# A new order for three chained stages, a mask made first, and three weight copies on another engine

## The chip, the cores and the metric

The kernel runs on one core of one Trainium2 chip. That core has TensorE (PE, matrix products into PSUM banks), VectorE (DVE), ScalarE (ACT), GpSimd (POOL) and SyncE (SP, which here only issues transfers); 16 DMA engines move data between HBM and the on-chip SBUF. The metric is the device time of the whole program in microseconds (us), the median of several executions. A time that goes down is an improvement.

## The reference

Three stages, the output of each the input of the next. The weights are float64, everything else float32.

```python
# attention: q, k, v of 4 x 8 x 576 x 64, a causal window of 64
scores = np.matmul(q, k.transpose(0, 1, 3, 2)) / np.sqrt(D)
mask = (rel >= 0) & (rel < 64)                       # rel = row - column
scores = np.where(mask, scores, -1e9)
attn = np.exp(scores - max); attn = attn / (sum + 1e-9)
x = np.matmul(attn, v)                               # -> 2304 x 512
# relu squared: 512 -> 2048 -> 512
h = np.maximum(x @ w_in, 0.0); x = h * h @ w_out
# SoLU: 512 -> 1024 -> 512
h = x @ w2_in
solu = h * softmax(h)
ln = (solu - mean) / np.sqrt(var + 1e-6) * g_ln
out = ln @ w2_out
```

## The kernel before

**Tiling.** The 2304 tokens are cut into blocks of 64. Two blocks make a *unit* of attention: a mask product and score products (`ps_s`, L417 and L436), the largest score of each row (`nmax`, L440 to L446, DVE), exponentials (`e`, L451, ACT), the division by the sums (L456 to L461), transposes (`ps_p`, L477 and L479), a copy (`pt`, L497, ACT) and the values (`ps_v`, L517 to L522). The feed-forward stage then goes through `ps_h` (L691, or L936 in later passes) and `ps_y` (L707, L1070, L1256). It works in passes over groups of tokens; the later passes and the third stage replace eight block products by seven, with sums and differences of blocks on DVE (`wf`, `y`, `g`, `gx`, `xx`, `ws`, `w2i`, `w2x`). Each float32 operand is split into a high and a low part, and each product is three products (high by high, high by low, low by high). The SoLU stage takes tokens in pairs of tiles: `pair2` makes `ps_h` at L1546 (42 matmuls of 512 columns for a pair), then the exponentials and the norm make `lnT` (L1696), and `ps_o` (L1707, 48 matmuls for a pair) gives the output, scaled and stored.

**Weights.** A block of float64 weights (128 x 512) comes by DMA as half-words (`wraw`, L236, issued by SP). A *half-word copy* moves each top half-word to its place in a zeroed buffer (`top`, a ring of two places for the feed-forward weights): by DVE (L263) for those with `i < TOPS`, else by ACT (L265). DVE then shifts the rest in (L268), ACT makes the high part (L284), DVE the low part (L287). The weights of the first product are called a0, a1, ... (`in_w_in`, then `wa`), those of the second b0, b1, ... (`in_w_out`, then `wb`). Products of the first pass can start when a0, its high and low parts and the first unit's values are there.

**Order.** Every piece of work is a task of a `Plan` (from L27): an engine, an estimated length, a rank, what it must follow, which buffers it takes and gives, and `late`, an allowance after its end (for a transfer, until its data can be used). `run` places on each step the task that can start first, and of these the one of lowest rank; a table `SHIFT` adds a number to the rank of single tasks. `emit` then writes the tasks in the order of their planned starts, and nothing is reordered afterwards: an engine that waits for one instruction holds up all that stand behind it on that engine, and the same is true of SP's and ACT's transfers. `late` and the table are numbers of the plan alone; they change no instruction, only places.

**Filling.** 51 matmuls of `ones` (`ps_warm`, L1782) have the highest rank of all, so that the plan puts them where it sees TensorE idle: 36 as one group, then 15 single ones. Their result isn't used.

**The start.** Constants are made first: `ident` and `mask` by POOL, `ident_b`, `lower` and `mask_b` by DVE (L175 to L183). `mask_b` goes into every mask product; `lower` is used from the third unit on. `top` is zeroed by POOL (L256), just before the first half-word copy needs it.

**The end.** The last output tile is scaled in two halves into two buffers, one by ACT (L1721), one by DVE (L1723), and each half is stored by a transfer of its own, one issued by SP and one by ACT (L1727). All other tiles are scaled whole by ACT (L1712).

Of the kernel before, what the change touches and what calls it, by code (L numbers as in the profile page):

```python
# [20 lines left out]
P = 128  # L21
# [5 lines left out]
class Plan:  # L27
# [10 lines left out]
    SHIFT = {0: 13.59, 3: 4.48, 4: -11.32, 22: -7.17, 37: 14.79, 71: -15.08, 162: -5.57, 188: 6.06, 192: -3.28, 195: 10.82, 198: 10.82, 202: -1.28,  # L38
# [69 lines left out]
def kernel(  # L108
# [68 lines left out]
    V.memset(mhalf, -0.5)  # L177
    lower = const.tile([P, 2 * BLK], F32, name="lower")
    V.tensor_scalar(out=lower, in0=mask, scalar1=0.0, scalar2=1e29, op0=ALU.min, op1=ALU.mult)
    mask_b = const.tile([P, 2 * BLK], BF16, name="mask_b")  # L180
    V.tensor_scalar(out=mask_b, in0=mask, scalar1=0.0, scalar2=8.0, op0=ALU.min, op1=ALU.mult)
    ident_b = const.tile([P, P], BF16, name="ident_b")
    V.tensor_copy(ident_b, ident)  # L183
# [21 lines left out]
    with ExitStack() as c1:  # L205
# [151 lines left out]
        def attention(n, rank, after=()):  # L357
# [186 lines left out]
            if n == 0:  # L544
                lqs = [add("SP", 1.1, rank - 6, lambda h=h: load_qk(h), take=qk * (h == 0), late=2.0, at=0.7) for h in range(2)]
# [300 lines left out]
        def w_operands(t, j, rank, after):  # L846
# [9 lines left out]
            def kept(o, k):  # L856
                nc.sync.dma_start(out=wo_dram[j][:, k], in_=o["t"].bitcast(F32))
# [48 lines left out]
            kept_wo[j] = [add("SP", 1.6, rank + WOS, lambda o=o, k=k: kept(o, k), [x], late=2.5) for k, (o, x) in enumerate(((V_, v), (Y, y)))]  # L906
# [5 lines left out]
        def pair1(t, j, at, unit, held, begins_after=()):  # L912
# [91 lines left out]
            for x, kk, f, k in (("c22", 2 * j + 1, f22, 6), ("u3", 2 * j, f21, 8)):  # L1004
                f = squared(Named({}, o, x), N, rank(k) + 14.3, [f], False, False)
                r_ready[t, kk] = add("SP", 0.8, rank(k) + 3, lambda x=x, kk=kk: store(x, kk), [f], late=LATE_R if t == 2 else 2.2, give=["wm"])
# [829 lines left out]
```

## Time and profile before

| | us |
|---|---|
| median of 3 executions | 630.67 (630.58 to 631.52) |
| the profiled execution's own time | 631.49 |
| its span, first to last instruction | 629.7 |
| TensorE busy in the span | 621.6 (99%) |
| VectorE busy | 484.6 (77%) |
| ScalarE busy | 434.8 (69%) |
| GpSimd busy | 45.3 (7%) |
| mean granted clock of TensorE | 1.000 |

The profiled execution took 631.49 us, of which 629.7 us lie between its first and its last instruction; the other 1.8 us lie around the span. Its own time is near the highest of the three others. Matmuls are pipelined and their ends are modelled, so rows of TensorE overlap a little: the distance between two starts says how long a group held the engine. In the trace a name in front of the arrow is what is written, the names behind it what is read; "idle before" is the engine's idle time ahead of an instruction, and the name behind it what came last. "SPq" is the queue of transfers that SP issues.

### The profile page before, as it was taken

Reading aid. Unit: us, or ns where it says so; the run is one execution under the profiler, and the core shown is the slowest. Engines: PE = TensorE matmul, PEld = TensorE weight load, DVE = VectorE, ACT = ScalarE, POOL = GpSimd, SP = SyncE. Lnnn points to the kernel's source line nnn. Section 1 sums busy time; section 2 is a strip of 40 time slices with the busy share of each in tenths; the row PEclk is TensorE's granted clock in tenths of the full one; section 3 lists DMA queues with packets and bytes.
Section 4 is the critical chain, followed back from the end, with each engine's and each line's share of the span. In section 5 each row is a group of like instructions: output and inputs, shape, how many; then the busy total and the mean of one; then the engine's idle time right before and its main releaser. Section 6 shows DMA issues by size and latency. Waiting matters only on the chain.

```text
span 629.7 us, 11572 instructions
## 1 busy us (share of the span) xinstructions
PE 621.6 (99%) x4009; PEld 523.7 (83%) x4009; DVE 484.6 (77%) x1129; ACT 434.8 (69%) x985; POOL 45.3 (7%) x80
## 2 busy tenths in 40 slices
PE   8999999999999999999999999999999999999998
PEld 4798878889999999998888887778778788888886
DVE  5999897497967652587899998998688976686440
ACT  5879785677877674638677767774688875776451
POOL 1000000001221110000000000000001010110010
DMA  8888979447899998946767557964166565532351
GB/s 274 287 305 278 310 252 326 128 173 264 247 351 312 336 304 271 337 155 230 236 251 263 203 195 235 328 208 138 68 184 206 181 199 167 197 137 86 116 184 50
DMA packets 85451, 141.27 MB, mean 224 GB/s; under 512 B 7824, under 2 KB 49552, under 8 KB 85392
## 3 DMA queue, kind: packets, MB, share of 16 engines
q1 hardware_dynamic: 84704, 140.14, 66.3%
q8 instruction: 31, 0.51, 0.3%
q10 hardware_dynamic: 688, 0.39, 0.2%
q14 instruction: 28, 0.23, 0.1%
HBM read 90.69 MB, written 49.81 MB: 223 GB/s over the span
## 4 chain that ended last, share of the span: by engine, by line
PE 86%; DVE 5%; DMA 4%; ACT 3%; issue 1%; SPq 1%; POOL 0%; ACTq 0%; DVEq 0%; POOLq 0%
PE ps_h L936 22%; PE ps_o L1707 14%; PE ps_y L1070 10%; PE ps_h L1546 10%; PE ps_y L1256 10%; PE ps_y L707 7%; PE ps_h L691 6%; PE ps_s L436 3%; PE ps_v L519 2%; PE ps_warm L1782 1%; DMA l<-t_dram 1%; DMA kt<-in_k 1%; DMA r_dram<-u 1%; DMA t_dram<-h 1%; PE ps_v L522 1%
## 5 line engine op out<-in xcount | busy, mean ns | idle before, releaser
L1707 PE MATMUL ps_o<-w2o,lnT 128*128 128x512 f32 x432 | 99.1, 389 | 0.0
L1707 PEld LDWEIGHTS ps_o<-w2o,lnT 128*128 128x128 f32 x432 | 81.1, 188 | 16.9
L1256 PE MATMUL ps_y<-g,wb 128*128 128x384 f32 x384 | 71.3, 336 | 0.4 <-ACT y L655 0.4
L1256 PEld LDWEIGHTS ps_y<-g,wb 128*128 128x128 f32 x384 | 66.6, 188 | 1.4 <-ACT y L655 0.7
L1546 PE MATMUL ps_h<-w2i,xx 128*128 128x512 f32 x243 | 62.8, 391 | 0.0
L1070 PE MATMUL ps_y<-g,wb 128*128 128x512 f32 x234 | 58.3, 391 | 1.1 <-DVE y L1157 1.0
L1546 PEld LDWEIGHTS ps_h<-w2i,xx 128*128 128x128 f32 x243 | 45.6, 188 | 9.6
L1070 PEld LDWEIGHTS ps_y<-g,wb 128*128 128x128 f32 x234 | 43.7, 188 | 11.4 <-DVE y L1157 1.4
L936 PE MATMUL ps_h<-xa,wo 128*128 128x512 f32 (+1 forms) x192 | 52.7, 369 | 0.0
L936 PE MATMUL ps_h<-xb,wo 128*128 128x384 f32 (+1 forms) x192 | 51.3, 358 | 0.0
L707 PE MATMUL ps_y<-g,wb 128*128 128x512 f32 (+1 forms) x240 | 48.2, 352 | 0.1
L691 PE MATMUL ps_h<-x,wa 128*128 128x512 f32 (+1 forms) x240 | 47.3, 351 | 0.0
L936 PE MATMUL ps_h<-xo,wo 128*128 128x512 f32 (+1 forms) x128 | 47.3, 369 | 0.0
L451 ACT ACTIVATE e<-e,nmax 128x128 f32<-128x128 f32 x112 | 43.3, 390 | 2.2 <-DVE nmax L440 2.2
L707 PEld LDWEIGHTS ps_y<-g,wb 128*128 128x128 f32 x240 | 38.5, 189 | 6.6 <-issue 0.7
L691 PEld LDWEIGHTS ps_h<-x,wa 128*128 128x128 f32 x240 | 38.5, 189 | 6.0 <-ACT g L637 0.2
L936 PEld LDWEIGHTS ps_h<-xa,wo 128*128 128x128 f32 x192 | 35.3, 188 | 5.2 <-DVE u L622 0.4
L1696 ACT ACTIVATE lnT<-l 128x512 fp32r<-128x512 f32 x36 | 22.2, 627 | 23.0 <-PE ps_o L1707 23.0
L1546 PE MATMUL ps_h<-w2x,xx 128*128 128x512 f32 x135 | 37.0, 393 | 0.9 <-ACT u L1560 0.7
L936 PEld LDWEIGHTS ps_h<-xb,wo 128*128 128x128 f32 x192 | 34.5, 188 | 3.9 <-issue 0.7
L640 DVE TENSOR_TENSOR g<-r,g 128x384 fp32r<-128x384 f32 (+2 forms) x36 | 20.4, 570 | 21.7 <-ACT g L637 21.7
L461 POOL TENSOR_TENSOR e<-e,sums 128x512 f32<-128x512 f32 x16 | 18.5, 1179 | 205.0 <-PE ps_h L936 141.9
(182 smaller groups left out, 1267.7 us busy)
## 6 DMA issues: line engine op xcount, KB each, us to landing
wraw<-in_w_in SPq DMA_DIRECT2D x24, 511.8 KB, 5.3
wraw<-in_w_out SPq DMA_DIRECT2D x24, 511.8 KB, 4.8
vt<-in_v SPq DMA_DIRECT2D x32, 256.0 KB, 4.3
wo_dram<-wo SPq DMA_DIRECT2D x16, 512.0 KB, 5.4
wo<-wo_dram SPq DMA_DIRECT2D x16, 512.0 KB, 4.9
t_dram<-h SPq DMA_DIRECT2D x16, 512.0 KB, 2.9
l<-t_dram SPq DMA_DIRECT2D x64, 128.0 KB, 2.9
kt<-in_k SPq DMA_DIRECT2D x16, 384.0 KB, 5.2
```

Source lines behind the costliest of these rows:

```text
L436: T.matmul(to, qt[rows, i, hp, :], kt[rows, keys, hp, :], start=not begins, stop=not begins or hp == hps[-1])
L451: S.activation(out=o["er"][:, a, w], in_=s, func=AF.Exp, scale=SCALE if begins else -1.0, bias=o["nmax"][:, a, w : w + 1], accum_out=o["su ...
L461: eng.tensor_tensor(out=o["er"][:, a], in0=o["er"][:, a], in1=o["sums"][:, a].unsqueeze(2).to_broadcast([P, HP, W]), op=ALU.mult)
L640: V.tensor_tensor(out=o["g"][:, 1, :N], in0=o["r"], in1=o["g"][:, 0, :N].bitcast(F32), op=ALU.subtract)
L691: T.matmul(ps[:, :N], wa[kk][:, wi, c * P : c * P + P], xs[t][:, xi, c, n0:n1], start=n == 0, stop=n == 3 * DC - 1)
L707: T.matmul(acc[t, 0][d][:, n0:n1], wb[kk][:, wi, d * P : d * P + P], o["g"][:, xi, :N], start=kk == 0 and n == 0 and n0 == 0, stop=last an ...
L936: T.matmul(to[:, :N], w["t"][:, wi, off + c * P : off + c * P + P], (lo if xi else hi)()[:, c], start=begins and m == 0, stop=m == 5, skip ...
L1070: T.matmul(acc[name][d][:, :N], wb[kk][:, wi, col + d * P : col + d * P + P], q["g"][:, xi, :N], start=j == 0 and n == 0 and name not in ( ...
L1256: T.matmul(acc[t, half][d][:, :N], wb[kk][:, wi, d * P : d * P + P], q["g"][:, xi, :N], start=pos == 0 and n == 0, stop=pos == KF - 1 and ...
L1546: T.matmul(o[bank], o["xx", k][:, xi, at : at + P], w2i[w, r][wi][0](), start=begins and m == 0, stop=m == 5, skip_group_check=True)
L1696: S.activation(out=parts2(o["l", hf][:, 0]), in_=turned2(hf), func=AF.Copy)
L1707: T.matmul(o["o"], o["l", hf][:, xi, kk % 4, :], w2o[kk][:, wi, :], start=kk == 0 and n == 0, stop=kk == KF2 - 1 and n == 2)
```

## The change

The function of the program is the same, and so are the counts of every form of matmul. What changes:

- **The table `SHIFT`** is replaced by another with half as many entries, and four kinds of `late` are changed (the loads of q and k of the first unit, and several stores). Together they put most of the work of all engines in another order.
- **Constants:** `ident_b`, `mask_b`, `lower` in that order, and `top` is created and zeroed up front, by DVE instead of POOL.
- **Half-word copies** of a0, a1 and b0 go from DVE to ACT. The place in the ring of `top` is now taken from a list of free ones and given back after the shift.
- **The end:** the last tile is scaled whole by ACT and stored in two halves, still by SP's and ACT's queues.

```diff
-    SHIFT = {0: 13.59, 3: 4.48, 4: -11.32, 22: -7.17, 37: 14.79, 71: -15.08, 162: -5.57, 188: 6.06, 192: -3.28, 195: 10.82, 198: 10.82, 202: -1.28,
+    SHIFT = {0: 23.49, 10: 1.29, 28: -4.64, 214: 8.42, 331: -39.05, 389: 14.27, 467: -9.61, 473: -42.13, 501: 3.17, 563: 26.76, 1037: -4.85,
...
+    ident_b = const.tile([P, P], BF16, name="ident_b")
+    V.tensor_copy(ident_b, ident)
+    mask_b = const.tile([P, 2 * BLK], BF16, name="mask_b")
+    V.tensor_scalar(out=mask_b, in0=mask, scalar1=0.0, scalar2=8.0, op0=ALU.min, op1=ALU.mult)
     lower = const.tile([P, 2 * BLK], F32, name="lower")
     V.tensor_scalar(out=lower, in0=mask, scalar1=0.0, scalar2=1e29, op0=ALU.min, op1=ALU.mult)
-    mask_b = const.tile([P, 2 * BLK], BF16, name="mask_b")
...
-        tops, turns = [], [0]
+        tops, turns = [x_p.tile([P, 2, 512], F32, tag="xc", name="top", bufs=1)], [0, 1]
+        V.memset(tops[0], 0.0)
...
-            by_dve = ringed and i < TOPS
+            by_dve = ringed and (1 if kind == "b" else 2) <= i < TOPS
...
-                    if not tops:
-                        tops.append(x_p.tile([P, 2, 512], F32, tag="xc", name="top", bufs=1))
-                        G.memset(tops[0], 0.0)
-                    o["t"] = tops[0][:, turns[0] % 2]
-                    turns[0] += 1
+                    o["turn"] = turns.pop(0)
+                    o["t"] = tops[0][:, o["turn"]]
...
+                if ringed:
+                    turns.append(o["turn"])
...
-                lqs = [add("SP", 1.1, rank - 6, lambda h=h: load_qk(h), take=qk * (h == 0), late=2.0, at=0.7) for h in range(2)]
+                lqs = [add("SP", 1.1, rank - 6, lambda h=h: load_qk(h), take=qk * (h == 0), late=1.8, at=0.7) for h in range(2)]
...
-                if b == 0:
-                    S.activation(out=o["y", b][:, cols], in_=o["o"][:, cols], func=AF.Copy, scale=o["rstd"])
-                else:
-                    V.tensor_scalar(out=o["y", b][:, cols], in0=o["o"][:, cols], scalar1=o["rstd"], scalar2=None, op0=ALU.mult)
...
+            a = add("ACT", 0.59, rank_o, scaled, [a, r], take=["r"], give=["a"])
             if k == 1 and p["last"]:
-                b = add("ACT", 0.35, rank_o, lambda: scaled_half(0), [a, r], take=["r"])
-                c = add("DVE", 0.35, rank_o, lambda: scaled_half(1), [a, r], take=["r"], give=["a"])
-                add("SP", 0.5, rank_o, lambda: store_half(0), [b], late=2.0, give=["r"])
-                add("ACT", 0.1, rank_o, lambda: store_half(1), [c], late=2.0, give=["r"])
+                add("SP", 0.5, rank_o, lambda: store_half(0), [a], late=2.0, give=["r"])
+                add("ACT", 0.1, rank_o, lambda: store_half(1), [a], late=2.0)
```

What this moves shows best in the order of instructions. The new kernel's line numbers are 4 lower from the constants on, and up to 14 lower at the end.

**SP's loads at the start.** Before, SP issues a0 (`in_w_in`), the v of unit 0, b0 (`in_w_out`), a1, then unit 2's q and k, a2, the v of unit 1:

```order
L236 DMA wraw<-in_w_in 128x2047
L401 DMA vt<-in_v 64x512 x2
L236 DMA wraw<-in_w_out 128x2047
L236 DMA wraw<-in_w_in 128x2047
L390 DMA qt<-in_q 128x512
L391 DMA kt<-in_k 128x768
L236 DMA wraw<-in_w_in 128x2047
L401 DMA vt<-in_v 64x512 x2
```

After:

```order
L233 DMA wraw<-in_w_out 128x2047
L397 DMA vt<-in_v 64x512 x4
L386 DMA qt<-in_q 128x512
L387 DMA kt<-in_k 128x768
L233 DMA wraw<-in_w_in 128x2047 x3
```

b0 is now first, both units' v follow it, then unit 2's q and k, and only then a0 with two more blocks of that kind.

**DVE in the middle, around 399 us of the profiled span.** `y` (L1157) takes a finished product from PSUM, `wb` (L1044) is a low part of a combined weight, `g` and `gx` are activations, `wf` the combining. Before:

```order
L1157 TENSOR_TENSOR y<-ps_y,y 128x512
L1035 TENSOR_TENSOR wf<-wf 128x256
L1036 TENSOR_TENSOR wf<-wf 128x256
L1037 TENSOR_TENSOR wf<-wf 128x256
L1038 TENSOR_TENSOR wf<-wf 128x256
L1094 TENSOR_TENSOR gx<-r,gx 128x512
L1094 TENSOR_TENSOR g<-r,g 128x512
L1044 TENSOR_TENSOR wb<-wf,wb 128x512 x2
L1157 TENSOR_TENSOR y<-ps_y,y 128x512
```

After:

```order
L1040 TENSOR_TENSOR wb<-wf,wb 128x512
L1153 TENSOR_TENSOR y<-ps_y,y 128x512 x2
L1090 TENSOR_TENSOR g<-r,g 128x512
L1090 TENSOR_TENSOR gx<-r,gx 128x512 x2
L332 TENSOR_TENSOR ws_4939<-w2i,ws_4740 128x512
```

The two `y` now stand together behind one `wb`; the second `wb`, which stood ahead of the second `y`, comes some 15 rows later.

**PE between the first pair of the SoLU stage and its output product.** Before, the first pair's L1546 ends, 12 matmuls of the last pass (L1070) follow, then 7 of `ones`, then the second pair:

```order
L1546 MATMUL ps_h_5249<-w2x,xx 128x512 x3
L1546 MATMUL ps_h_5249<-w2i,xx 128x512 x3
L1070 MATMUL ps_y<-g,wb 128x512 x6
L1070 MATMUL ps_y<-gx,wb 128x512 x6
L1782 LDWEIGHTS ones
L1782 MATMUL ps_warm<-ones 128x512
...
L1546 MATMUL ps_h_5363<-w2i,xx 128x512 x3
L1546 MATMUL ps_h_5363<-w2x,xx 128x512 x3
```

After, from the last L1066 (the old L1070) on: the first pair (`ps_h_5269`), the second (`ps_h_5349`), 9 matmuls of `ones`, the third (`ps_h_5483`):

```order
L1066 MATMUL ps_y<-gx,wb 128x512 x6
L1542 MATMUL ps_h_5269<-w2i,xx 128x512 x3
...
L1542 MATMUL ps_h_5349<-w2i,xx 128x512 x3
...
L1542 MATMUL ps_h_5349<-w2x,xx 128x512 x3
...
L1768 LDWEIGHTS ones
L1768 MATMUL ps_warm<-ones 128x512
...
L1542 MATMUL ps_h_5483<-w2i,xx 128x512 x3
```

All of L1070 now stands ahead of the first pair, the second pair follows the first without anything between, and the matmuls of `ones` stand between the second pair and the third. Over the whole program the 51 matmuls of `ones` stand, before: 36 ahead of the first L691, 3 at the start of the last stretch of L1070, 7 and 1 around the second pair, 4 behind the last `ps_o`. After: 32 ahead of the first L691, 9 among the first products that follow it (4, 1, 2 and 2), 1 in the stretch of L1070, 9 behind the second pair, none at the end.

## Rows read from the trace of the kernel before

**Rows 1.** The page: length, and the busiest engines.

```profile
span 629.7 us, 11572 instructions
PE 621.6 (99%) x4009; PEld 523.7 (83%) x4009; DVE 484.6 (77%) x1129; ACT 434.8 (69%) x985; POOL 45.3 (7%) x80
```

**Rows 2.** Timeline of DVE and POOL, start: start, us, engine, line, operation.

```profile
0.81 0.17 DVE L175 MEMSET ones<- 128x128 bf16 x1 [0.81 <-PEq L1826]
0.93 0.06 DVE L177 MEMSET mhalf<- 128x1 f32 x1
...
2.42 0.98 DVE L181 TENSOR_SCALAR mask_b<-mask 128x128 bf16<-128x128 f32 x1
...
2.30 0.95 POOL L256 MEMSET top<- 128x1024 f32 x1
```

**Rows 3.** Timeline of PE, start to the first L691.

```profile
3.45 0.58 PE L417 MATMUL ps_s<-mask_b,ident_b 128*128 128x128 bf16 x4 [0.52 <-DVE mask_b L181]
...
8.12 0.46 PE L436 MATMUL ps_s<-qk 64*64 64x64 f32 x16 [0.19 <-DMA qk<-in_k]
...
21.38 0.82 PE L691 MATMUL ps_h<-x,wa 128*128 128x256 f32 x4
```

**Rows 4.** Timeline of SP (a0, unit 2's q, a2) and of DVE (first half-word copy).

```profile
2.75 0.47 SPq L236 DMA_DIRECT2D wraw<-in_w_in  x1
...
6.76 0.33 SPq L390 DMA_DIRECT2D qt<-in_q  x1
...
8.00 0.33 SPq L236 DMA_DIRECT2D wraw<-in_w_in  x1
...
10.49 0.46 DVE L263 CAST top<-wraw 128x512 f16<-128x512 bf16 x1
```

**Rows 5.** Busy by stretch: us, PE, PEld, DVE, ACT, POOL (instructions), clock, DMA share, GB/s.

```profile
3.00:16.00 13.00, 11.83 (x188) 6.91 (x188) 8.44 (x29) 7.32 (x40) 0.25 (x1) 1.00 0.98 318
20.00:35.00 15.00, 14.90 (x173) 13.15 (x161) 14.61 (x38) 13.01 (x47) 0.00 (x0) 1.00 0.86 308
```

**Rows 6.** Half-word copies by shape: DVE's from 9 to 50 us, ACT's from 220 to 380 us.

```profile
L263 DVE CAST top<-wraw 128x512 f16<-128x512 bf16 x14 | 6.4, 456 | 0.3 <-DMA wraw<-in_w_out 0.3
L265 ACT ACTIVATE wm<-wraw 128x512 f16<-128x512 bf16 x8 | 6.3, 782 | 0.2 <-POOL wm L249 0.2
```

**Rows 7.** Timeline of PE, the scores of the sixth unit.

```profile
45.17 1.22 PE L436 MATMUL ps_s<-kt,qt 64*64 64x128 f32 x32 [0.39 <-DMA kt<-in_k]
```

**Rows 8.** Timeline of PE, then of DVE, around 399 us.

```profile
388.06 0.82 PE L1782 MATMUL ps_warm<-ones 128*128 128x512 bf16 x3
...
401.42 1.66 PE L1070 MATMUL ps_y<-g,wb 128*128 128x512 f32 x6 [0.98 <-DVE y L1157]
...
399.48 1.28 DVE L1044 TENSOR_TENSOR wb<-wf,wb 128x512 fp32r<-128x512 f32 x2
400.69 0.68 DVE L1157 TENSOR_TENSOR y<-ps_y,y 128x512 f32<-128x512 f32 x1
```

**Rows 9.** Timeline of PE from the first pair's end to the first output product.

```profile
444.80 1.52 PE L1070 MATMUL ps_y<-g,wb 128*128 128x512 f32 x6
446.16 1.52 PE L1070 MATMUL ps_y<-gx,wb 128*128 128x512 f32 x6
447.52 2.12 PE L1782 MATMUL ps_warm<-ones 128*128 128x512 bf16 x7
...
468.33 0.96 PE L1546 MATMUL ps_h<-w2x,xx 128*128 128x512 f32 x3 [0.70 <-ACT u L1560]
...
469.82 2.43 PE L1707 MATMUL ps_o<-w2o,lnT 128*128 128x512 f32 x10
```

**Rows 10.** Timeline of all engines at the end; then ACT's scaling of whole tiles.

```profile
626.09 0.47 ACT L1721 ACTIVATE o<-ps_o,rstd 128x256 f32<-128x256 f32 x1 [4.80 <-PE ps_o L1707]
...
627.11 0.36 ACTq L1727 DMA_DIRECT2D out<-o  x1
...
L1712 ACT ACTIVATE o<-ps_o,rstd x17: 667/672/690, 478.5 to 620.6; 128x512 f32<-128x512 f32 x17
```

More of the change, by code (lines that the diff above doesn't have):

```diff
@@ L177 @@
     V.memset(mhalf, -0.5)
+    ident_b = const.tile([P, P], BF16, name="ident_b")
+    V.tensor_copy(ident_b, ident)
+    mask_b = const.tile([P, 2 * BLK], BF16, name="mask_b")
+    V.tensor_scalar(out=mask_b, in0=mask, scalar1=0.0, scalar2=8.0, op0=ALU.min, op1=ALU.mult)
     lower = const.tile([P, 2 * BLK], F32, name="lower")
     V.tensor_scalar(out=lower, in0=mask, scalar1=0.0, scalar2=1e29, op0=ALU.min, op1=ALU.mult)
-    mask_b = const.tile([P, 2 * BLK], BF16, name="mask_b")
-    V.tensor_scalar(out=mask_b, in0=mask, scalar1=0.0, scalar2=8.0, op0=ALU.min, op1=ALU.mult)
-    ident_b = const.tile([P, P], BF16, name="ident_b")
-    V.tensor_copy(ident_b, ident)
     gcol = const.tile([P, 152], F32, name="gcol")[:, :KF2]
@@ L905, in w_operands @@
             z = cut(Z, lambda: units()[:, 3], 256, have)
-            kept_wo[j] = [add("SP", 1.6, rank + WOS, lambda o=o, k=k: kept(o, k), [x], late=2.5) for k, (o, x) in enumerate(((V_, v), (Y, y)))]
+            kept_wo[j] = [add("SP", 1.6, rank + WOS, lambda o=o, k=k: kept(o, k), [x], late=3.0) for k, (o, x) in enumerate(((V_, v), (Y, y)))]
             return named(u, v, y, z, [u, v2, v4, z])
@@ L1005, in pair1 @@
                 f = squared(Named({}, o, x), N, rank(k) + 14.3, [f], False, False)
-                r_ready[t, kk] = add("SP", 0.8, rank(k) + 3, lambda x=x, kk=kk: store(x, kk), [f], late=LATE_R if t == 2 else 2.2, give=["wm"])
+                r_ready[t, kk] = add("SP", 0.8, rank(k) + 3, lambda x=x, kk=kk: store(x, kk), [f], late=LATE_R + 0.45 if t == 2 else 2.2, give=["wm"])
             for x, kk, f, slot, k, seconds in (("c11", 2 * j, f11, "r", 1, (10, 11) if lastj else (10, 13)), ("c12", 2 * j + 1, f12, "wm", 9, (12, 13) if lastj else (16, 19))):
@@ L1133, in blocks_of @@
             l4 = parted(lambda: o["c12"], N, rank(13), [c], g["T4"], give=["wm"])
-            kept_t[j, "T1"] = add("SP", 0.8, r + 3, lambda: store("u3", r_dram[t][2 * j]), [b], late=2.2, give=["wm"])
-            kept_t[j, "B22"] = add("SP", 0.8, r + 3, lambda: store("c22", r_dram[t][2 * j + 1]), [b], late=2.2, give=["ws"])
-            kept_t[j, "T"] = add("SP", 1.6, r + 3, lambda: store("tt", tt_dram[j].rearrange("p k n -> p (k n)")), [c], late=2.5, give=["raw"])
+            kept_t[j, "T1"] = add("SP", 0.8, r + 3, lambda: store("u3", r_dram[t][2 * j]), [b], late=2.65, give=["wm"])
+            kept_t[j, "B22"] = add("SP", 0.8, r + 3, lambda: store("c22", r_dram[t][2 * j + 1]), [b], late=2.65, give=["ws"])
+            kept_t[j, "T"] = add("SP", 1.6, r + 3, lambda: store("tt", tt_dram[j].rearrange("p k n -> p (k n)")), [c], late=3.4, give=["raw"])
             p = [times("P1", j, 2 * j, 0, g["B11"], l11, rank(8), take=["b"] * (j == 0), give=["g"], after=gone[t - 1, 0, 0] if j == 0 else []),
@@ L1715, in store_o @@
                 nc.sync.dma_start(out=out[i * P : i * P + P, :], in_=o["y"])
-            def scaled_half(b):
-                cols = slice(256 * b, 256 * b + 256)
-                o["y", b] = g_p.tile([P, NMAX], F32, tag="r", name="o", bufs=3)
-                if b == 0:
-                    S.activation(out=o["y", b][:, cols], in_=o["o"][:, cols], func=AF.Copy, scale=o["rstd"])
-                else:
-                    V.tensor_scalar(out=o["y", b][:, cols], in0=o["o"][:, cols], scalar1=o["rstd"], scalar2=None, op0=ALU.mult)
             def store_half(b):
                 cols = slice(256 * b, 256 * b + 256)
-                (nc.scalar if b else nc.sync).dma_start(out=out[i * P : i * P + P, cols], in_=o["y", b][:, cols])
+                (nc.scalar if b else nc.sync).dma_start(out=out[i * P : i * P + P, cols], in_=o["y"][:, cols])
             a = add("ACT", 1.10, rank, exp_h, done, take=["wb"])
@@ L1755, in behind @@
                 l_free[k, hf] = [a]
+            a = add("ACT", 0.59, rank_o, scaled, [a, r], take=["r"], give=["a"])
             if k == 1 and p["last"]:
-                b = add("ACT", 0.35, rank_o, lambda: scaled_half(0), [a, r], take=["r"])
-                c = add("DVE", 0.35, rank_o, lambda: scaled_half(1), [a, r], take=["r"], give=["a"])
-                add("SP", 0.5, rank_o, lambda: store_half(0), [b], late=2.0, give=["r"])
-                add("ACT", 0.1, rank_o, lambda: store_half(1), [c], late=2.0, give=["r"])
+                add("SP", 0.5, rank_o, lambda: store_half(0), [a], late=2.0, give=["r"])
+                add("ACT", 0.1, rank_o, lambda: store_half(1), [a], late=2.0)
                 return
-            a = add("ACT", 0.59, rank_o, scaled, [a, r], take=["r"], give=["a"])
             add("SP", 1.0, rank_o, store_o, [a], late=2.0, give=["r"])
```

12 rows, old and new, of the table SHIFT are left out of this document.

## The prediction

> **What bounds the kernel now.** I read the page first: TensorE is busy 621.6 of 629.7 us [rows 1]. It computes the same matmuls before and after, and the 51 matmuls of `ones` stay 51. So the time changes only where TensorE idles, or runs `ones` in place of idling, and by what lies ahead of its first and behind its last matmul. Then I read the places where a row of PE has an idle time in front of it, or where `ones` stands: the start, the first products, the region around 399 us, the first pairs of the SoLU stage, the end. There a reader should see who came last: DVE's `mask_b` before the first mask product and the transfer of k before unit 1's scores [rows 3], a late k at 45 us [rows 7], a `y` on DVE at 401 us [rows 8], ScalarE at 468 us [rows 9]. DVE is no bound over the span (77%), but it is in the stretch from 20 to 35 us: 14.61 of 15 us busy, while PE is busy 14.90 [rows 5]. The profiled execution took 631.49 us against a median of 630.67, 0.82 more. All terms below are differences within that execution; I apply their sum to the median.
>
> **The start.** Before, DVE's `mask_b` takes 0.98 us for 128 columns, though `ones`, as large, takes 0.17; it ends at 3.40, just after POOL's memset of `top` (2.30 to 3.25) [rows 2]. I read this as one engine held by the other. The change puts that memset on DVE, ahead of `ident_b` and `mask_b`. No DVE memset of 1024 columns is in the trace. From 0.06 us for one column and 0.17 for 128 [rows 2], 0.0009 us per further column gives 0.95 us; eight times 0.17 gives 1.36. Starting at 0.99 it ends at 1.94 to 2.35; `ident_b` and `mask_b` follow at about 0.17 each, `mask_b` not before POOL's mask (2.27), so at 2.4 to 2.7. The first mask product starts at 2.5 to 2.8 instead of 3.45: 0.65 to 0.95 us earlier. I take 0.9. Unit 0's exponentials follow by as much. Unit 1's scores don't: they wait at 8.12 for their k [rows 3], which no edit loads earlier. So nothing of this reaches the products by itself.
>
> **The loads.** The first L691 at 21.38 [rows 3] waits for the last of: unit 1's values, and a0 with its two parts. The change loads unit 1's v together with unit 0's, which frees the first. But a0 is issued at 2.75 before [rows 4]; after, b0, both v and unit 2's q and k stand ahead of it on SP. It takes the place that a2 has before, at 8.00, since unit 2's q (6.76) waits for unit 0's buffers [rows 4], perhaps 0.5 earlier with the earlier mask. From issue to the first half-word copy a0 took 10.49 - 2.75 = 7.7 us, and the DMA engines were busy 0.98 of that stretch [rows 5]; so a0 is usable at 15.2 to 15.7. The Trainium skill, page "DMA: Bandwidth & Descriptors", section "Queues, rings and completion order", says that on each DMA engine the descriptors of a ring are consumed in order. By that rule a0 is late by the 1,664 KB put ahead of it (b0 512, v 512, q 256, k 384), an estimate of 5.2 us at the 318 GB/s of that stretch, and would be usable at 15.7; the sum would not change by it.
>
> From there a0 needs a copy on ScalarE (0.78), where DVE took 0.46 [rows 6], and then the shift, the high and the low part, about 0.68 each (128x512, as a `y` on DVE [rows 8]): 2.8 us, and queueing behind exponentials on ScalarE and divisions on DVE, for which I take 2 to 3. The first L691 then starts at 19.9 to 21.4; I take 20.4, a gain of 1.0. Queued behind a0's copy on ScalarE are unit 2's exponentials: 3 copies of 0.78 add 2.3 us there, and take 3 x 0.46 = 1.4 us from DVE, which is the fuller of the two in that stretch [rows 5]. The 9 matmuls of `ones` among the next products cost up to 0.27 each (0.82 for 3 [rows 8]), 2.4 us, if the holes that the plan sees are real or not; part of it before would be idle time that the pipeline's modelled ends hide. I take 1.8. The late k at 45 us (0.39 idle [rows 7]) should go, since q and k of that unit are issued earlier. **Head: -1.0 + 1.8 - 0.4 = +0.4**, from -1.0 (half of the `ones` stand in holes that were there) to +1.5.
>
> **Around 399 us.** Before, PE waits 0.98 us for the second `y`, which stands on DVE behind two `wb` of 1.28 us together [rows 8]. After, one `wb` stands ahead of both `y`. That takes 0.6 us from the wait; the second `wb` comes 15 rows later, and its product waits for it only if these rows are late. What is then late next is the `y` itself, with 0.3 us left. The 3 matmuls of `ones` at 388 us (0.82) become 1. **-0.6 and -0.5**, together from -1.3 to 0.
>
> **The pairs.** From 444.80 to 469.82 PE holds 12 matmuls of L1070 and 84 of L1546. Two groups of 6 start 1.36 us apart, 0.227 us for one [rows 9]: 96 x 0.227 = 21.8 of 25.0 us. The other 3.2 us are 8 matmuls of `ones` and waits, 0.70 of it for ScalarE at 468.33 [rows 9]. After, the 12 are done ahead of the first pair, and 9 of `ones` at some 0.22 to 0.27 (2.0 to 2.4 us) are the only filling: if no wait is added, 0.8 to 1.2 us are gained. If the wait at 468.33 stays, 0.1 to 0.5. I take **-0.7**, with bounds -1.2 and +0.5 (the second pair, now directly behind the first, needs the banks that DVE empties, as the `ones` before it show).
>
> **The end.** Before, the second half's store is issued at 627.11, behind ACT (626.09, 0.47) and then DVE [rows 10]. After, one ACT instruction of 0.67 ends at 626.76 and both stores follow: **-0.3**. It could be no gain if both stores share what one had alone; -0.35 to 0.1.
>
> **The sum.** +0.4 - 1.1 - 0.7 - 0.3 = -1.7. The table moves work in all other passes as well, where PE has hardly an idle time to lose. A new order can only add waits there: 0 to 1.5, and I take 0.3. That leaves -1.4: 630.67 - 1.4 = 629.3. A measurement of this kernel can tell some 0.2%, 1.26 us, from no change, so "faster" begins at 629.4.
>
> **The rivals.**
>
> *The plan's gain turns into other waits (no change).* The place is the pairs: the 9 `ones` in front of the third pair say that the plan sees 2 us of idle there, as much as in front of the second pair before. If the wait for ScalarE stays too, the pairs give 0 instead of -0.7, and if the second `wb` is missed 15 rows later, the region around 399 us gives -0.5 instead of -1.1. The sum is then -0.4 - 0.3 + the 0.3 to 0.6 of new waits: 630.3 to 630.7. For it: DVE is busy in the middle just as before. Against it: the rows name `y` and L1560, and `y` does move ahead.
>
> *a0 is late (slower).* If a0's low part ends after the 21.4 at which L691 starts now, the head's gain of 1.0 is gone and each further 1 us costs 1 us, as PE has nothing but `ones` until then. With a0 usable at 15.7, 2.8 for copies and parts, and the queueing at its upper end of 3, it is 21.5; a third instruction of 0.7 to 0.9 in its way makes 22.4. The head is then +0.4 + 1.0 + 1.0 = +2.4, the sum +0.3 to +0.6, and with 1 us of new waits in a fuller ScalarE 632.0. For it: DMA at 0.98, and 13 `ones` directly ahead of the first L691. Against it: DVE and ScalarE are through with unit 1 earlier, and free for a0.
>
> *The holes are real (faster by more).* The `ones` of the head then cost nothing that PE would not have idled; the head gives -1.0, the sum -2.8: 627.9. This is the near end of my forecast's own case.
>
> **How the numbers follow.** Forecast, faster, 627.6 to 629.4: 0.47, with 629.3 as the sum gives it. Waits that turn into others, 629.4 to 631.9: 0.31. A late a0 or new waits in the rest, above 631.9: 0.22. The range from 627.7 to 632.3 leaves out 1 in 10 above and a little below; its upper end is the slower rival's 632.0 with 0.3 of new waits.
>
> **What would show it.** Right: first mask product before 2.9; first L691 between 19.9 and 21.0; no idle of 0.3 or more for k near 45 us; the wait for `y` around 399 us below 0.5; from the first pair's end to the first L1707 at most 21.9 us (before 25.0, less the 2.7 of L1070, 22.3); the last store issued at about 0.7 us behind the last `ps_o`. Wrong: a first L691 after 21.4 with an idle time for a0's parts in front of it; a new idle time above 0.5 us on PE between 50 and 390 us; or `ones` in front of the third pair and still a wait for ScalarE behind them.

## The result and the profile after

The changed kernel takes 636.12 us (median of 6 runs, 634.44 to 637.36), the kernel before 630.66 (6 runs): 1.0084 times as long, 95% interval 1.0073 to 1.0095, or 5.5 us. I had forecast 629.3 and a range of 627.7 to 632.3. The profiled execution took 636.89 us, with a span of 635.1.

The page of the changed kernel, as [rows 1]:

```profile
span 635.1 us, 11581 instructions
PE 622.0 (98%) x4009; PEld 524.5 (83%) x4009; DVE 482.8 (76%) x1126; ACT 436.4 (69%) x988; POOL 44.2 (7%) x79
```

TensorE does the same work in as much busy time; what came on top is idle time and, as will be seen, a lower clock. To find the place, count the matmuls of each trace in time order, by form and by the tiles that they write and read, and leave `ones` out. Both traces hold 3958 of them, of every form as many, so the two can be compared at each point where both kernels have done exactly the same ones:

| time in the kernel before, us | the changed kernel is behind by, us |
|---|---|
| 20.5 (first product of the changed kernel) | -1.0 |
| 23.0 | 0.3 |
| 38.8 | 2.6 |
| 83 to 241 | 2.0 to 2.1 |
| 264 to 279 | 1.3 |
| 295.2 | 1.0 |
| 303.3 | 2.3 |
| 384.7 | 2.2 |
| 418.9 | 0.5 |
| 423.0 | 2.0 |
| 449.3 | 0.3 |
| 459.1 | 1.8 |
| 468.3 | 5.7 |
| 506 to the end | 5.4 |

So three stretches lose for good: the first 40 us (2.6, of which 0.5 comes back), 295 to 303 us (1.3), and above all that of the pairs (some 2.1 behind when they begin, 5.7 at the first output product). Between 241 and 295 us 1.0 is gained, and two places gain and lose again: around 400 us, and within the pairs.

The start of TensorE, as [rows 3] (start, us, engine, line, operation):

```profile
3.02 0.58 PE L413 MATMUL ps_s<-mask_b,ident_b 128*128 128x128 bf16 x4
...
7.93 0.46 PE L432 MATMUL ps_s<-qk 64*64 64x64 f32 x16 [0.76 <-DMA qk<-in_k]
...
19.52 0.58 PE L687 MATMUL ps_h<-x,wa 128*128 128x256 f32 x2
20.55 1.46 PE L687 MATMUL ps_h<-x,wa 128*128 128x256 f32 x10 [0.45 <-DVE wa L283]
```

The mask is 0.4 us earlier, unit 1's scores wait for k as before, and the first product starts 1.9 us earlier (1.0 at equal work). Then it waits for a0's low part: between the second and the third matmul of L687 0.8 us are lost.

TensorE around the third pair, as [rows 9], and DVE beside it:

```profile
459.12 2.12 PE L1768 MATMUL ps_warm<-ones 128*128 128x512 bf16 x9
460.88 1.05 PE L1542 MATMUL ps_h<-w2i,xx 128*128 128x512 f32 x3
461.77 0.84 PE L1542 MATMUL ps_h<-w2x,xx 128*128 128x512 f32 x3
464.44 3.70 PE L1542 MATMUL ps_h<-w2i,xx 128*128 128x512 f32 x9 [1.83 <-DVE nmax L1571]
467.93 1.79 PE L1542 MATMUL ps_h<-w2x,xx 128*128 128x512 f32 x6
...
473.99 0.96 PE L1542 MATMUL ps_h<-w2x,xx 128*128 128x512 f32 x3 [0.85 <-ACT u L1556]
...
475.48 4.70 PE L1703 MATMUL ps_o<-w2o,lnT 128*128 128x512 f32 x20
```

```profile
459.96 0.68 DVE L1571 CUSTOM_DVE_ANT_0 h<-ps_h,u 128x512 f32<-128x512 f32 x1
...
460.57 0.71 DVE L1660 STREAM_TRANSPOSE h<-e 128x512 f32<-128x512 f32 x1
461.20 0.65 DVE L1520 TENSOR_TENSOR xx<-xs,xx 128x512 fp32r<-128x512 f32 x1
461.77 0.70 DVE L1660 STREAM_TRANSPOSE h<-e 128x512 f32<-128x512 f32 x1
462.39 0.65 DVE L1520 TENSOR_TENSOR xx<-xs,xx 128x512 fp32r<-128x512 f32 x1
462.96 0.74 DVE L1571 CUSTOM_DVE_ANT_0 h<-ps_h,u,nmax 128x512 f32<-128x512 f32 x1
...
463.63 0.75 DVE L1571 CUSTOM_DVE_ANT_0 h<-ps_h,u,nmax 128x512 f32<-128x512 f32 x1
```

The last of these rows is `c12` of the second pair, the sum that reads the last bank of a tile of PSUM that the third pair writes. TensorE, which has run 9 matmuls of `ones` and the third pair's first product, waits 1.83 us until it has ended. In the kernel before `c12` stands ahead of the second pair's `c22`, and the second product starts without a wait (DVE, then PE):

```profile
459.31 0.74 DVE L1575 CUSTOM_DVE_ANT_0 h<-ps_h,u,nmax 128x512 f32<-128x512 f32 x1
...
459.98 0.68 DVE L1575 CUSTOM_DVE_ANT_0 h<-ps_h,u 128x512 f32<-128x512 f32 x1
...
460.65 2.22 PE L1546 MATMUL ps_h<-w2i,xx 128*128 128x512 f32 x9
```

In the new order it stands behind `c22`, two transposes, two parts of `xx` and `c21`. Behind the wait 9 matmuls take 3.49 us (464.44 to 467.93) where 9 x 0.227 = 2.0 are usual [rows 9]. The stretches say why (us, then PE, PEld, DVE, ACT, POOL busy, then the granted clock):

```profile
462.00:464.00 2.00, 0.61 (x3) 0.18 (x1) 2.00 (x5) 1.44 (x3) 0.19 (x1) 1.00 0.94 268
464.00:466.00 2.00, 1.56 (x5) 1.30 (x6) 1.59 (x4) 2.00 (x4) 0.55 (x1) 0.76 0.62 248
466.00:468.00 2.00, 2.00 (x7) 1.54 (x6) 0.00 (x0) 1.49 (x4) 0.00 (x0) 0.50 0.27 75
468.00:470.00 2.00, 2.00 (x9) 1.64 (x8) 0.80 (x4) 0.10 (x1) 0.00 (x0) 0.88 0.82 221
```

After the idle time the granted clock falls to 0.50, which is the lower of its two levels, 1.2 GHz, and is back at 2.4 by 470 us. At equal work the wait itself cost 2.0 us (1.8 behind ahead of it, 3.8 after it) and the slow stretch another 1.6 (5.4 behind at its end). This is the profiled execution, with a mean clock of 0.997; of the six executions three have 0.997 (635.81 to 637.36 us) and three 1.000 (634.44 to 636.43 us). So the lower clock follows in some executions and not in all.

Around 297 us (DVE, then PE):

```profile
295.90 0.69 DVE L1110 TENSOR_TENSOR tt<-c,u 128x512 f32<-128x512 f32 x1 [2.28 <-DMA x_dram<-y]
296.62 0.69 DVE L1113 TENSOR_TENSOR u<-u,p 128x512 f32<-128x512 f32 x1
297.24 0.68 DVE L618 CUSTOM_DVE_ANT_0 p<-ps_h,p 128x512 f32<-128x512 f32 x1
...
297.97 0.50 PE L932 MATMUL ps_h<-xb,wo 128*128 128x512 f32 x1 [0.24 <-DVE p L618]
```

DVE stands idle for 2.28 us in front of `tt`, whose buffer a store still reads, and `p`, which TensorE needs, stands behind it.

The region around 399 us, as [rows 8] (PE, then DVE):

```profile
398.66 1.43 PE L1066 MATMUL ps_y<-g,wb 128*128 128x512 f32 x5 [0.80 <-DVE g L1090]
...
422.14 1.42 PE L1066 MATMUL ps_y<-gx,wb 128*128 128x512 f32 x5 [0.96 <-DVE gx L1090]
...
397.58 0.42 DVE L1034 TENSOR_TENSOR wf<-wf 128x256 f32<-128x256 f32 x1
397.92 0.68 DVE L1090 TENSOR_TENSOR g<-u,g 128x512 fp32r<-128x512 f32 x1
```

The wait for `y` is gone; in its place TensorE waits 0.80 us for a `g` that stands behind the four `wf`, and 0.96 us for a `gx` at 422. The gain was there, 2.2 us behind at 385 and 0.5 at 419 us, and was gone again at 423.

The end, as [rows 10]:

```profile
631.51 0.69 ACT L1708 ACTIVATE o<-ps_o,rstd 128x512 f32<-128x512 f32 x1 [4.80 <-PE ps_o L1703]
632.23 0.33 SPq L1715 DMA_DIRECT2D out<-o  x1
632.23 0.37 ACTq L1715 DMA_DIRECT2D out<-o  x1
```

From the first scaling to the last store's issue 0.72 us pass instead of 1.02 (627.11 less 626.09). But that store lands 2.03 us after its issue (634.26) where it took 1.72 before (628.83), so that from the first scaling to the last landing 2.75 us pass, and 2.74 before.

### The profile page after: what moved, and what is told of

The parts are those of the page before. It is cut to its first block, busy times and chain, and to the rows that moved or that the text cites. A ratio compares the mean times of both kernels' runs of the same rounds, so it can differ in the third digit from the quotient of the medians.

```text
span 635.1 us, 11581 instructions
## 1 busy us (share of the span) xinstructions
PE 622.0 (98%) x4009; PEld 524.5 (83%) x4009; DVE 482.8 (76%) x1126; ACT 436.4 (69%) x988; POOL 44.2 (7%) x79
## 4 chain that ended last, share of the span: by engine, by line
PE 84%; DVE 6%; DMA 4%; ACT 3%; issue 1%; SPq 0%; ACTq 0%; DVEq 0%
PE ps_h L932 19%; PE ps_o L1703 15%; PE ps_h L1542 13%; PE ps_y L1252 10%; PE ps_y L703 7%; PE ps_h L687 7%; PE ps_y L1066 6%; DMA r<-tt_dram 2%; PE ps_s L432 2%; PE ps_v L515 2%; PE ps_v L518 1%; DVE g L1090 1%; DMA x_dram<-y 1%; DMA qk<-in_k 1%; PE ps_p L475 1%
## 5 line engine op out<-in xcount | busy, mean ns | idle before, releaser
L1542 PE MATMUL ps_h<-w2i,xx 128*128 128x512 f32 x243 | 64.3, 398 | 1.8 <-DVE nmax L1571 1.8
L1066 PE MATMUL ps_y<-g,wb 128*128 128x512 f32 x234 | 57.8, 391 | 0.8 <-DVE g L1090 0.8
L1066 PEld LDWEIGHTS ps_y<-g,wb 128*128 128x128 f32 x234 | 43.8, 188 | 10.5 <-DVE g L1090 1.5
L687 PE MATMUL ps_h<-x,wa 128*128 128x512 f32 (+1 forms) x240 | 48.2, 353 | 0.8 <-DVE wa L283 0.4
L687 PEld LDWEIGHTS ps_h<-x,wa 128*128 128x128 f32 x240 | 38.6, 189 | 8.5 <-issue 0.9
```

The costliest lines, as they stand in the source:

```text
L687: T.matmul(ps[:, :N], wa[kk][:, wi, c * P : c * P + P], xs[t][:, xi, c, n0:n1], start=n == 0, stop=n == 3 * DC - 1)
L1066: T.matmul(acc[name][d][:, :N], wb[kk][:, wi, col + d * P : col + d * P + P], q["g"][:, xi, :N], start=j == 0 and n == 0 and name not in ( ...
L1542: T.matmul(o[bank], o["xx", k][:, xi, at : at + P], w2i[w, r][wi][0](), start=begins and m == 0, stop=m == 5, skip_group_check=True)
```

## The experiments

The theory I formed from these rows (A): single instructions that the new table puts late hold TensorE up, `c12` most of all. Rivals: (B) the order loses in many places and a wait removed comes back behind it; (C) the edits themselves, above all the copies on ScalarE, make the loss. The instructions are written out in the plan's order, so an edit of that list moves one of them and leaves all others. Tasks are named by their number in the plan.

**`c12` first.**

```diff
         self.order = sorted(done, key=lambda t: t["start"])
+        early, before = (next(t for t in done if t["n"] == n) for n in (1840, 1842))
+        self.order.remove(early)
+        self.order.insert(self.order.index(before), early)
```

> One DVE instruction of the changed kernel moves and nothing else: c12 of the second pair, the sum that reads the last bank of ps_h that the third pair's third product needs, goes from behind c22, two transposes, two parts of xx and c21 to directly ahead of c22. In the changed kernel TensorE waits 1.83 us for it at 464.44 and then runs 3.4 us at a granted clock of 0.5. Theory A (this late instruction makes most of the loss): the wait is gone, the clock stays 1.00, 1.8 + 1.7 = 3.5 us less than the changed kernel where the clock fell, 2 to 2.5 us less in the median, some 633.5. Rival B (the new order loses in many places, a wait removed here comes back behind it): less than 1 us gained, 635.2 to 636. Rival C (the edits of the start and the copies make the loss): no gain, 636.

633.78 us (633.23 to 635.27, 7 runs), 2.3 less. TensorE, third pair:

```profile
461.62 2.20 PE L1545 MATMUL ps_h<-w2i,xx 128*128 128x512 f32 x9
463.66 0.84 PE L1545 MATMUL ps_h<-w2x,xx 128*128 128x512 f32 x3
465.14 0.96 PE L1545 MATMUL ps_h<-w2x,xx 128*128 128x512 f32 x3 [0.64 <-ACT p L1551]
...
470.72 0.96 PE L1545 MATMUL ps_h<-w2x,xx 128*128 128x512 f32 x3 [1.18 <-ACT u L1559]
```

The 9 matmuls take 2.0 us again (461.62 to 463.66), and no slow ones follow; the mean clock is 0.999 or 1.000 in all 7 executions. Part comes back as waits for ScalarE (0.64 and 1.18 in place of 0.85), as B says. One DVE instruction was 2.3 of the 5.5 us.

**`ones` behind, and then in, the wait.** Two runs add 8 matmuls of `ones` to the changed kernel: behind task 1891, the third pair's second product, and behind 1889, its first.

```diff
         for t in self.order:
             t["fn"]()
+            if t["n"] == 1889:
+                for _ in range(8):
+                    self.fill()
```

> The changed kernel with 8 more matmuls of ones between the second and the third product of the third pair, where TensorE idles 1.83 us before it runs at the lower clock. The wait itself stays, the engine is busy in it. If the lower clock follows from the idle time, the clock stays 1.00 behind it and 1.7 us are gained in the executions that had the lower clock, with a median of 634.5 to 635.5. If the clock falls for another reason, it falls again and the time is 636 or, with 8 matmuls of 0.21 beyond the wait, up to 0.3 more.

> The earlier run put its 8 matmuls of ones behind the second product of the third pair, but the wait is ahead of that product, so that they only added 2.4 us. Here the 8 stand between the first and the second product, in the 1.83 us wait itself. If the lower clock behind the wait follows from the idle time, the clock stays 1.00 in every execution and the median falls to 634 to 635. If not, 636 as the changed kernel.

Behind the second product: 638.54 us, 2.4 more; I had put them on the wrong side of the wait, and they ran at the lower clock. In the wait: 634.18 us (633.68 to 635.66, 4 runs), 1.9 less than the changed kernel. In the wait's stretch and behind it:

```profile
461.43 1.90 PE L1771 MATMUL ps_warm<-ones 128*128 128x512 bf16 x8
463.39 2.33 PE L1545 MATMUL ps_h<-w2i,xx 128*128 128x512 f32 x9
```

```profile
464.00:466.00 2.00, 2.00 (x10) 1.66 (x9) 0.55 (x1) 2.00 (x4) 0.00 (x0) 1.00 0.15 61
466.00:468.00 2.00, 2.00 (x10) 1.67 (x9) 1.38 (x5) 1.17 (x4) 0.00 (x0) 1.00 0.82 246
```

Nothing but the idle time was filled, and the clock stayed at 1.00 here and at 0.999 or 1.000 in all 4 executions, so the lower clock followed from the idle time. What it cost is less sure than the 1.9 us: in the profiled execution 1.6 by equal work, but half of the changed kernel's executions did not have it, and their median (635.80) is above 634.18 too.

**The second product written out ahead of `c12`.** Task 1891 goes ahead of 1840, with the same lines as above; each engine's order is the same.

> No engine's order changes here: only the place in the program's text at which the third pair's second product is written out goes ahead of c12. c12 reads bank c, the second product writes bank b, both in one tile of two banks. If the product's wait for c12 is a wait for the tile and not for the bank, it goes: TensorE then runs the second product (1.4 us) before it waits for c12 ahead of the third, the wait shrinks from 1.83 to some 0.5 us or, if c12 now waits for the product in turn, to about 1, and the clock may stay up: 633.5 to 635.5. If the product needed c12 for another reason, nothing changes: 636.

633.99 us (633.34 to 634.76, 4 runs), 2.1 less:

```profile
461.70 1.53 PE L1545 MATMUL ps_h<-w2i,xx 128*128 128x512 f32 x6
464.17 0.93 PE L1545 MATMUL ps_h<-w2i,xx 128*128 128x512 f32 x3 [0.94 <-DVE nmax L1574]
```

The second product runs without a wait, the third waits 0.94 us, and the clock stays up. So the second product had waited for a read of the other bank of its tile. The plan keeps the two banks apart, the program's waits don't: the plan saw no wait where there is one, and put 9 `ones` into a hole that lay elsewhere.

**The edits, undone one by one in the new order.** The copies of a0, a1, b0 by DVE at the same places, and the start of before.

```diff
-                if by_dve:
+                if by_dve or (ringed and i < TOPS):
                     V.tensor_copy(to, word)
```

> The changed kernel in its own order, but the half-word copies of a0, a1 and b0 are done by DVE at the same place (0.46 us each on DVE in place of 0.78 on ScalarE). My prediction gave the copies no sign of their own, only a later a0 part by 0.3 us. Theory A: the first L691 starts within 0.5 us of 19.5, and the total stays within 0.6 of 636. Rival C (the copies on ScalarE hold up the exponentials and with them the head): the first 40 us become 1 to 1.5 us shorter and the total 634.6 to 635.

> The changed kernel with the start of before: top zeroed by GpSimd, lower and mask_b ahead of ident_b. If one of GpSimd and DVE holds the other, mask_b ends at 3.3 to 3.4 again and the first mask product starts at 3.45 (3.02 in the changed kernel). The total: theory A and my prediction both say that nothing of the start reaches the first L691, because unit 1's k comes at 7.9 in any case, so within 0.4 of 636. A rival: the earlier exponentials of unit 0 let unit 1's values and a0's parts start earlier, and the first L691 is 0.4 us later, as the mask.

635.98 us (632.55 to 637.52, 7 runs) and 636.65 (636.02 to 636.93, 4 runs): no difference that these runs can tell. In the first the 12 matmuls of L687 start at 19.68 and run without the wait for a0's low part, yet at 83 us that kernel is 2.2 us behind all the same. In the second the first mask product starts at 3.45 again, the first L687 at 19.98, 0.46 later as its rival has it. But with the new start the first L687 lies between 19.35 and 19.98 from run to run (19.98 where unit 1's scores start at 8.39), so these single traces don't tell whether the start reaches it.

**The edits alone, in the old order.** First start and end, then with the copies on ScalarE.

> The kernel before, in its own order, with two of the edits: the start (top zeroed by DVE up front, mask_b ahead of lower) and the end (the last tile scaled whole by ScalarE, stored in two halves). My prediction gave the end 0.3 us and the start nothing that reaches the products: 630.3 to 630.7, so no difference that three rounds can tell, with mask products 0.4 us earlier and the last store 0.3 us earlier behind the last ps_o. A rival: the end's two stores now share the queue and their landing is later, then 630.9 or more.

> All edits of the change (start, end, the copies of a0, a1 and b0 on ScalarE) at the places of the old order; the table and the planner's allowances are the old ones, nothing is reordered. Theory A (the order makes the loss, the edits are worth little): within 0.5 us of the kernel before, 630.2 to 631.2. Rival C (the copies on ScalarE cost the head its time): 1 us or more above, 631.6 or more, with a first L691 after 21.9.

630.64 us (10 runs; before 630.81; ratio 0.9998, 0.9989 to 1.0007) and 631.05 (12 runs; before 630.77; 1.0007, 0.9996 to 1.0017). In the profiled executions the first L691 starts at 20.94 with start and end, and at 21.70 with the copies too, against 21.38 before: that fits a cost of the copies there, which the time doesn't show. C falls: the edits are worth nothing that these runs can tell, 1.1 us at most (the upper end of the second interval); the order makes the loss.

**The tables exchanged.** The changed kernel with the old table and allowances, and the kernel before with the new ones; the plan places everything anew.

```diff
-    SHIFT = {0: 23.49, 10: 1.29, 28: -4.64, 214: 8.42, 331: -39.05, 389: 14.27, 467: -9.61, 473: -42.13, 501: 3.17, 563: 26.76, 1037: -4.85,
+    SHIFT = {0: 13.59, 3: 4.48, 4: -11.32, 22: -7.17, 37: 14.79, 71: -15.08, 162: -5.57, 188: 6.06, 192: -3.28, 195: 10.82, 198: 10.82, 202: -1.28,
...
```

> The changed kernel with the old table and the old allowances; the planner places the edits' tasks anew, so that the old table, whose numbers were found for the old tasks, now gives a third order. If the new table as such were bad, the old one would give some 631. If any table only fits the tasks it was found for, this order loses too, by 1 to 4 us: 632 to 635. I expect the second.

> The kernel before with the new table and the new allowances, without the edits; the planner gives a fourth order. If the table only fits the tasks it was found for, this is slower than the kernel before by 1 to 5 us, 632 to 636, and for waits in other places than in the changed kernel. If the new table as such is good and the edits hurt, some 630.

634.98 and 648.69 us (4 runs each). The first is within the 632 to 635 expected, the second far outside of 632 to 636. Either table loses with tasks for which it wasn't found, by 4 and 18 us; neither says which table is better as such. Where the 18 us are lost wasn't taken apart.

**Without the early `ones`, then without the late ones too.** As `c12` first, and 9, then 18 of the `ones` are not issued.

```diff
         for t in self.order:
+            if 2335 <= t["n"] <= 2343:
+                continue
             t["fn"]()
```

> As the run with c12 put first (633.78 us), and the 9 matmuls of ones that stand among the first products behind the first L687 (4, 1, 2, 2) are left out; they are no part of the result. Compared at equal amounts of done products, the changed kernel falls behind the kernel before by some 1.9 us between its 26th and its 50th microsecond, where these 9 stand, and still has about 1 of it at 60. If they take time from the products (my prediction took 1.8 of their 2.4 as a cost), the time falls by 1 to 2 us to some 632. If they only fill holes (the rival with real holes), the products start no earlier and the time stays within 0.4 of 633.8.

> c12 first, and neither the 9 matmuls of ones among the first products nor the 9 in front of the third pair. With c12 first TensorE waits only for the parts of the third pair's xx there. If the 9 fill a hole, the time is that of the run without the first 9, 632.8, or up to 1.7 more where the idle time lowers the clock. If they hold up the third pair, which by DVE's rows has its first part at 458.9 while the first product starts at 460.1, up to 1.1 less: 631.7.

632.79 us (631.76 to 635.37, 8 runs), 1.0 less than with them, about half of their 2.0 us; the other half would then be holes. At 83 us the kernels with these 9 are 2.1 and 1.9 us behind the kernel before at equal work (changed, and `c12` first), those without them 0.4 to 1.2. Without the 9 ahead of the third pair 634.04, 1.25 more. There TensorE idles 1.97 us, and the clock falls again (the mean clock is 0.997 in 3 of 4 executions):

```profile
464.45 0.98 PE L1547 MATMUL ps_h<-w2x,xx 128*128 128x512 f32 x3 [1.97 <-ACT p L1553]
```

```profile
466.00:468.00 2.00, 2.00 (x6) 1.52 (x5) 1.90 (x6) 1.97 (x5) 0.00 (x0) 0.50 0.74 224
```

So the late ones are worth their time as they keep the clock up, the early ones aren't.

**The sum ahead of the wait for a store.** As 632.79, with `t3` and `t1` (the rows of `tt` and `u` at 295.90 and 296.62) behind the sum `p`.

```diff
+        for n in (1167, 1166):
+            late, behind = (next(t for t in done if t["n"] == m) for m in (n, 1194))
+            self.order.remove(late)
+            self.order.insert(self.order.index(behind) + 1, late)
```

> As the run with c12 first and without the 9 early matmuls of ones (632.79), and in the block around 296 us the two instructions t3 and t1 of DVE go behind the sum c11 that stands behind them. t3 waits 2.28 us for a store that still reads its buffer, and TensorE waits for c11. If that wait is the cause of the 1.2 us that the changed kernel loses between 297 and 304 us, the time falls by 0.5 to 1.2: 631.6 to 632.3. If what TensorE lacks there is made by other instructions too, less than 0.4: 632.4 to 632.8.

631.90 us (631.14 to 634.32, 10 runs), 0.9 less. DVE:

```profile
294.39 0.69 DVE L627 CUSTOM_DVE_ANT_0 p<-ps_h,p 128x512 f32<-128x512 f32 x1 [1.53 <-ACT g L1096]
295.00 0.68 DVE L1119 TENSOR_TENSOR tt<-c,u 128x512 f32<-128x512 f32 x1
```

`p` starts 2.15 us earlier than in the run that this one changes (296.54 there), in the time in which DVE had waited 2.42 us for the store.

**The last product ahead of the copy of the other bank.** The wait for `u` in the third pair is in both kernels (0.70 at 468.33 in [rows 9]). In the old order with start and end, and then with all repairs of the new order:

```diff
+        for n in range(1778, 2259, 60):
+            product, copy = (next(t for t in done if t["n"] == m) for m in (n + 3, n))
+            self.order.remove(product)
+            self.order.insert(self.order.index(copy), product)
```

> The kernel before with the new start and end, and in each pair of the SoLU stage the last product (into bank a) is written out ahead of u4, the copy that reads bank d of the same tile; no engine's order changes. If the 0.70 us wait for ScalarE at 468.33 in the kernel before is a wait for the tile, it goes, and the time is 0.5 to 0.8 below the run with start and end alone (630.64): 629.8 to 630.2. If it is a wait for the data of bank a, nothing changes: 630.6.

> All repairs of the new order together: c12 first, no early ones, t3 and t1 behind the sum, in each pair the last product written out ahead of u4, and in the third pair the copy p ahead of an instruction of ScalarE that waits 2.3 us for DVE. The waits of 0.64 (for p) and 1.18 us (for u4) in the third pair should go: 1.0 to 1.8 below the run before it, 630 to 631.3, so level with the kernel before. If the waits come back as one for another instruction, some 632.

In the old order the wait for `u` goes, but the next thing late takes its place:

```profile
468.80 0.50 PE L1709 MATMUL ps_o<-w2o,lnT 128*128 128x512 f32 x1 [1.21 <-ACT lnT L1698]
```

631.22 us (11 runs; before 630.65; ratio 1.0005, 0.9996 to 1.0014): nothing gained. In the new order 630.74 us (630.12 to 633.28, 12 runs; ratio to before 1.0003, 0.9994 to 1.0012), 1.2 less than the run before it. That run holds two steps, the last products and the copy `p` ahead of an instruction that waits; which of them gave it wasn't taken apart. Its trace is of its slowest execution (633.28 us): the wait for `p` in the third pair is gone and that for `u` is 0.16 us, but in the fourth pair TensorE waits 2.66 us for `p`, behind an `lnT` that waited for a load, and the clock falls to 0.50 again. So B's warning holds there, though not in the median.

The steps from the changed kernel back to level:

| kernel | us | step |
|---|---|---|
| changed | 636.12 | |
| `c12` first | 633.78 | -2.3 |
| and no early `ones` | 632.79 | -1.0 |
| and the sum ahead of the wait for a store | 631.90 | -0.9 |
| and the waits for the other bank, and for ScalarE's `p` | 630.74 | -1.2 |
| before | 630.65 | |

The four steps are all of the 5.5 us. Against the executions of the kernel before that were taken beside them, the ratios are 1.0084, 1.0042, 1.0031, 1.0016 and 1.0003, each within 0.0009 to 0.0013. So `c12` and the sum of the other three are clear; the single sizes of these three are rough, as neighbours overlap. No version ran below the kernel before by more than these runs can tell.

## Why the prediction was wrong

- **Start: nearly right.** The mask product was forecast 0.65 to 0.95 us earlier and came 0.43 earlier. That GpSimd's memset had held `mask_b` fits: without it `mask_b` takes 0.23 us, with the old start 0.98 again. That nothing of it reaches the time held as far as the runs can tell.
- **Loads: right in kind, and better than forecast.** a0 landed at 14.71 us, forecast usable at 15.2 to 15.7; the first L687 came at 19.52, ahead of the range of 19.9 to 21.4. At equal work the changed kernel is 1.0 us ahead there, as the -1.0 says. The late k at 45 us is gone, as forecast.
- **Head: too small.** +0.4 forecast with an upper bound of +1.5, 2.1 measured at 83 us. The gain of 1.0 is spent at once, 0.3 behind at 23 us, by the first 4 `ones` and the wait for a0's low part (0.8), for which the sum had no term; but without that wait, with the copies on DVE, the kernel is as late at 83 us. All 9 `ones` cost 1.0 by the run without them, for which I had taken 1.8. What makes the rest stays open. The near bound was also added up wrongly: with all `ones` in holes it is -1.0 - 0.4 = -1.4, not -1.0, and the rival with real holes gives 627.5.
- **Around 399 us: the gain came and went.** I took -1.1 because one wait goes. Fewer `ones` and the missing wait for `y` did give 1.7 (2.2 behind at 385 us, 0.5 at 419), but `g` with 0.80 and `gx` with 0.96 us, which had moved too, were late next, and not `y` with 0.3. At 423 us it is 2.0 behind: the term was nearly nothing.
- **The pairs: this step failed.** -0.7 forecast, bounds -1.2 to +0.5; measured +3.6 (some 2.1 behind when they begin, 5.7 at 468 us). I counted what stands on TensorE between the pairs and took the plan's 9 `ones` for the size of the hole. The gain in front of the second pair came (0.3 behind at 449 us); the 9 `ones` in front of the third took 1.5 of it back, the wait for `c12` 2.0 more, the slow clock 1.6. I had named "the banks that DVE empties" as a danger and not looked up where on DVE the sums stand that empty them. The order showed `c12` six places later; at 0.7 us an instruction that is over 3 us. And a price was missing: idle time in front of full work cost nearly as much again through the clock.
- **The rest: right by luck.** 0.3 taken, 0.2 net between 83 and 385 us. The sum had neither the 1.3 lost at 295 to 303 us (the wait for the store, 0.9 by the run without it) nor the 1.0 gained between 241 and 295 us, whose cause stays open.
- **End: wrong.** -0.3 forecast, nothing measured. The last store is issued 0.3 us earlier and takes 0.3 us longer to land, so that the last landing is no earlier; "no gain if both stores share what one had alone" stood in the prediction as the other case.
- **Rivals.** "The plan's gain turns into other waits" had the place right (in front of the third pair) and the size wrong, 0 instead of 3.6; its sign came, `ones` in front of the third pair and a wait for ScalarE (0.85 us) behind them. "a0 is late", to which I gave the chance of slower, did not happen.

Added up, 2.1 us at 83 us, 0.2 up to 385, -0.2 around 399, 3.6 in the pairs, -0.2 between them and 506 us and nothing at the end are, but for rounding, the 5.4 between the spans.

## What to carry to other kernels

When a change reorders engines, follow for each place that must not wait all instructions that release it, above all the last readers of its PSUM tile, and not only the engine's own row. A plan that tracks buffers more finely than the program's waits do promises overlaps that don't exist. A table of shifts found for one list of tasks lost 4 and 18 us here when it was put to another. In a stretch where TensorE is the bound, price a wait with the slower clock that can follow it (2.0 and 1.6 us here); filler matmuls paid in a real wait (1.9 us) and cost 1.0 us where products were ready. And follow a store to its landing, not only to its issue.

## What was not expected of the hardware

A 1.83 us wait was followed by the lower of TensorE's two clock levels in the profiled execution (by the mean clock in 3 of 6), a 1.97 us wait in another kernel (in 3 of 4), and a 2.66 us wait in the slowest execution of a third. Of the four kernels that keep the first of these waits (the changed one, both undone edits, `ones` behind the second product) 15 of 21 executions have a mean clock of 0.997 or less; of the three in which it is gone, filled or cut to 0.94, none of 15 has.

GpSimd's work on the mask, in the changed kernel, beside DVE's memset of `top`; the last row is the same select in the kernel before:

```profile
1.15 0.91 DVE L223 MEMSET top<- 128x1024 f32 x1 [0.16 <-issue]
...
2.74 0.23 DVE L177 TENSOR_SCALAR mask_b<-mask 128x128 bf16<-128x128 f32 x1 [0.60 <-POOL mask L167]
...
1.54 0.69 POOL L167 TENSOR_SCALAR_AFFINE_SELECT mask<-mask 64x64 f32<-64x64 f32 x1
...
1.54 0.23 POOL L171 TENSOR_SCALAR_AFFINE_SELECT mask<-mask 64x64 f32<-64x64 f32 x1
```

A select that takes 0.23 us when the memset is on GpSimd took 0.69 while DVE's memset ran, and `mask_b` waited for it; the mask product came at 3.02 where the forecast has about 2.55. The same holds in the traces of the other runs, with the memset on either engine. Only this select is longer: the two ahead of it, at 1.11 and 1.36 us, run beside the memset too and take their usual 0.29 and 0.23. What holds the third one isn't shown. The Trainium skill, page "SBUF — State Buffer", section "Who interferes with whom", says that a DVE instruction with at most one SBUF input, outside the modes that use two ports, does not contend with GpSimd. The memset has no SBUF input; if it ran outside those modes, this trace doesn't agree, and the 0.69 stands.
